# First dense product in Strassen's block form as a stage of its own; queries next; second dense product last

## The chip, the cores and the metric

The kernel runs on one core of a Trainium2 chip. The metric is the device time of one execution in microseconds (us), lower is better. The engines are named as in the profile: PE (TensorE, matmuls), DVE (VectorE), ACT (ScalarE), POOL (GpSimd) and SP (the queue that issues the DMAs).

## The reference

Input x has 2048 rows and 640 columns. Two branches are mixed row by row with a gate; everything is float32.

```python
g = sigmoid((x * gate_w).sum(-1, keepdims=True))
# branch a: 32 heads of 20
q, k, v = split(x @ wqkv)
pq, pk = per_head(q, w_phi), per_head(k, w_phi)
phi_q = concat(softmax(pq), softmax(-pq))        # the same for phi_k
kv, z = phi_k^T v, phi_k summed over the rows
a = (phi_q kv / (phi_q z + 1e-6)) @ wo
# branch b
b = silu(x @ w1) @ w2                            # 640 -> 1728 -> 640
out = g * a + (1 - g) * b
```

`x @ w1` is the first dense product, the one with `w2` the second.

## The kernel before

Everything is held transposed: a tile has 128 features (partitions) by 512 rows of x, and the 640 columns of x are 5 chunks of 128. A float32 operand is split into a high part (`split`: a cast on ACT) and a low part (a subtraction on DVE or POOL), and each product is made in three passes (`PASSES`): high x high, high x low, low x high. `w1` has 13 full tiles of 128 features and 64 columns left over, which are stacked as high and low parts and need two passes.

The order of the instructions on PE, DVE, ACT and POOL is written out by hand: inside `inorder(...)` each of these engines keeps the order of the program text. DMAs are issued by SP, in an order that the scheduler chooses.

1. *Keys and values*: 16 tiles of 128 rows. `kv_proj` (L468) projects, `k_spikes`, `k_sums` and `k_split` make the key features, `kv_acc` (L438) and `kv_rest` (L449) sum features times values. Banks `kvp[0]` to `kvp[2]` hold the projection. The weights of the dense products are loaded and split beside it (`load_f`).
2. *Opening of the dense products*: beside tile 15, `h_first` (L531) makes four feature tiles of the first block in `kvp[0]` and `kvp[1]`; then `kv_out` writes the key-value sums out and the gates are made.
3. *Both dense products, block by block*: four blocks of 512 rows. `h_tile` (L515) makes one tile of the first product (15 matmuls) and its SiLU; two tiles later `out_acc` (L697) uses it in five accumulators of the second product. The result times 1-g goes to DRAM (`fb_d`).
4. Beside the last block: query weights (`fused`), tables, and four tiles of queries (12 to 15): `q_proj` (L426), the features `q_feat`, the sums `q_sum` and `q_norm_sum` on DVE, `q_norm` (L790) and `q_mul` (L826) on POOL, small steps in `q_small`.
5. *Steps*: for pairs of query tiles, `t_mm` (L963) transposes, `t_out` (L979) copies to SBUF, `n_mm` (L1031) makes the numerators, `w_mm` (L1069) the product with `wo`, `w_out` adds `fb_d` and stores. `step(u)` interleaves this with the queries of the following tiles. `PB` is the order of the pairs.

## Time and profile before

| | |
|---|---|
| median of 3 runs | 753.37 us (753.12 to 755.64) |
| profiled execution | 753.52 us, span of its trace 751.7 us |
| granted TensorE clock | 1.000 |
| PE busy | 745.9 us, 4187 matmuls |
| DVE, ACT, POOL busy | 345.1, 262.9, 258.8 us |
| moved by DMA | 50.38 MB, mean 67 GB/s |

By stages, from the profile's windows: keys and values to 173.7 us; the opening to 190; the dense products to about 581, the last 51 us of them with queries beside; the steps to the end, 170.7 us. The stages have different limits, so a share of the whole span says little about one of them. The groups of instructions give the mean duration of one instruction, the chain gives the times at which work followed work. A matmul's duration is longer than the distance from it to the next, since matmuls overlap.

### The profile page before, as it was taken

The page shows a single profiled execution, that of the slowest core. Times are in us where ns is not written, and L with a number is a line of the kernel's source. Part 1 is how long each engine was busy: PE and PEld are TensorE (multiplying, and loading weights), DVE is VectorE, ACT ScalarE, POOL GpSimd, SP SyncE. Part 2 cuts the span into 40 slices and gives each one's busy share as a digit, 9 for nine tenths or more (in the row PEclk, how much of TensorE's full clock was granted, in tenths as well). Part 3 has the DMA queues.
Part 4 walks back from the last instruction along what each step waited for, and adds up shares of the span by engine and source line. Part 5 has one row for each costly group of instructions (what it writes and reads, how often), then busy time and mean ns, then how long its engine had stood idle before and what let it go on. Part 6 is the DMA issues. An engine that isn't in the chain of part 4 may idle for free.

```text
span 751.7 us, 10464 instructions
## 1 busy us (share of the span) xinstructions
PE 745.9 (99%) x4187; PEld 649.2 (86%) x4187; DVE 345.1 (46%) x613; ACT 262.9 (35%) x478; POOL 258.8 (34%) x160
## 2 busy tenths in 40 slices
PE   9999999999999999999999999999999999999998
PEld 7888888888888888888888888888897999999997
DVE  5676666676651230112210122123278776776732
ACT  5444433346452311123111221133354434444231
POOL 2488777866200000000000000001057687776540
PEclk9999999999999999999999999999999999999999
DMA  8111111103660130001300025014002233121222
GB/s 258 53 54 53 54 53 54 58 16 102 185 204 14 37 118 1 1 0 53 105 0 1 0 50 142 35 37 139 15 1 97 78 106 101 57 70 44 72 84 79
DMA packets 35500, 50.38 MB, mean 67 GB/s; under 512 B 3545, under 2 KB 23273, under 8 KB 35451
## 3 DMA queue, kind: packets, MB, share of 16 engines
q1 hardware_dynamic: 35162, 49.19, 21.0%
q8 instruction: 33, 0.54, 0.3%
q10 hardware_dynamic: 288, 0.51, 0.3%
q14 instruction: 17, 0.13, 0.1%
HBM read 38.58 MB, written 11.11 MB: 66 GB/s over the span
## 4 chain that ended last, share of the span: by engine, by line
PE 95%; POOL 2%; DVE 1%; ACT 1%; issue 1%; DMA 1%; SPq 0%; POOLq 0%
PE acc L697 25%; PE ph L515 23%; PE kvp L468 16%; PE pa L1069 9%; PE pq L426 8%; PE pn L1031 3%; PE kv L438 3%; PE pT L963 2%; PE kvp L531 2%; PE kvp L327 1%; PE kvq L327 1%; PE pwk L316 1%; PE pwq L236 1%; POOL eq L826 1%; DMA wvr<-wv 1%
## 5 line engine op out<-in xcount | busy, mean ns | idle before, releaser
L122 POOL TENSOR_TENSOR xb<-xrb,xb 128x512 fp32r<-128x512 f32 (+1 forms) x18 | 20.2, 1147 | 322.1 <-ACT xb L120 322.1
L697 PE MATMUL acc<-u,w 128*128 128x512 f32 x480 | 114.2, 391 | 0.2 <-DVE u L122 0.2
L122 DVE TENSOR_TENSOR u<-ph,u 128x512 fp32r<-128x512 f32 x48 | 33.2, 691 | 175.8 <-ACT u L120 175.7
L697 PEld LDWEIGHTS acc<-u,w 128*128 128x128 f32 x480 | 89.6, 188 | 19.1 <-DVE u L122 0.6
L515 PE MATMUL ph<-xf,w 128*128 128x512 f32 x420 | 99.3, 389 | 0.0
L517 ACT ACTIVATE ph<-ph 128x512 f32<-128x512 f32 x48 | 27.9, 582 | 190.8 <-PE ph L515 190.7
L468 PE MATMUL kvp<-wh,xa 128*128 128x500 f32 (+1 forms) x420 | 93.3, 358 | 0.0
L515 PEld LDWEIGHTS ph<-xf,w 128*128 128x128 f32 x420 | 78.8, 188 | 16.3
L468 PEld LDWEIGHTS kvp<-wh,xa 128*128 128x128 f32 x420 | 71.5, 188 | 10.0
L1069 PE MATMUL pa<-oT,wo 128*128 128x256 f32 x600 | 77.8, 283 | 0.0
L1069 PEld LDWEIGHTS pa<-oT,wo 128*128 128x128 f32 x600 | 74.2, 189 | 0.8 <-ACT oT L1040 0.8
L697 PE MATMUL acc<-u,f 128*128 128x512 f32 x300 | 71.8, 390 | 0.0
L515 PE MATMUL ph<-xf,f 128*128 128x512 f32 x300 | 71.3, 389 | 0.0
L515 PEld LDWEIGHTS ph<-xf,f 128*128 128x128 f32 x300 | 56.3, 188 | 11.7
L697 PEld LDWEIGHTS acc<-u,f 128*128 128x128 f32 x300 | 56.2, 188 | 11.6
L790 POOL TENSOR_TENSOR ez<-eq,zbc 128x1280 f32<-128x1280 f32 x16 | 47.1, 2946 | 41.1 <-ACT eq L776 41.1
L122 POOL TENSOR_TENSOR ph<-ek,ph 128x1280 fp32r<-128x1280 f32 x16 | 47.4, 2962 | 28.5 <-ACT ph L120 28.5
L426 PE MATMUL pq<-wq,xb 128*128 128x320 f32 x360 | 55.9, 312 | 0.0
L426 PEld LDWEIGHTS pq<-wq,xb 128*128 128x128 f32 x360 | 52.8, 188 | 2.3 <-issue 1.2
L468 PE MATMUL kvp<-wl,xa 128*128 128x500 f32 (+1 forms) x210 | 47.6, 356 | 0.0
L826 POOL TENSOR_TENSOR eq<-eq,sm 128x1280 f32<-128x1280 f32 x16 | 37.9, 2370 | 23.6 <-DVE sm L820 19.9
L468 PEld LDWEIGHTS kvp<-wl,xa 128*128 128x128 f32 x210 | 36.3, 189 | 5.5
(154 smaller groups left out, 1026.0 us busy)
## 6 DMA issues: line engine op xcount, KB each, us to landing
wr<-w SPq DMA_DIRECT2D x26, 320.0 KB, 3.4
xrf<-xT SPq DMA_DIRECT2D x20, 256.0 KB, 4.0
fb_d<-o SPq DMA_DIRECT2D x20, 256.0 KB, 2.4
y<-fb_d SPq DMA_DIRECT2D x16, 256.0 KB, 3.2
out<-y SPq DMA_DIRECT2D x16, 256.0 KB, 2.4
xra<-xT SPq DMA_DIRECT2D x14, 256.0 KB, 2.7
xrb<-xT SPq DMA_DIRECT2D x12, 256.0 KB, 2.6
wo<-wo SPq DMA_DIRECT2D x5, 320.0 KB, 2.8
```

The source lines that it names most:

```text
L122: eng.tensor_tensor(lo, src, hi.bitcast(F32), op=ALU.subtract)
L327: nc.tensor.matmul(kv_cols(t, lo, hi), x_of(t)[c][:, hx, :], WKV[hw][:, c, lo:hi], start=(opens and hx == 0 and hw == 0), stop=(c == NC - ...
L426: nc.tensor.matmul(dst, xt[c][:, hx, :], w[:, c, hw, lo : lo + n], start=first, stop=(hx == 1 and c == NC - 1))
L438: nc.tensor.matmul(kvt[i // 2][: KF + 1, i % 2], vs[t % VB][:, i, : KF + 1], ph[:, :, ks[i] : ks[i] + P], start=(t == 0 and i % 2 == 0), s ...
L468: nc.tensor.matmul(kv_cols(t, lo, hi), xt[c][:, hx, :], WKV[hw][:, c, lo:hi], start=(n == 0), stop=(n == 3 * NC - 1), skip_group_check=True,)
L515: nc.tensor.matmul(ph, lhs, rhs, start=(n == 0), stop=(n == len(todo) - 1))
L517: nc.scalar.activation(hs, ph, AF.Silu)
L697: nc.tensor.matmul(acc[m], lhs, rhs, start=(f == order[0] and n == 0), stop=(f == order[-1] and n == len(todo) - 1))
L790: nc.gpsimd.tensor_tensor(ez, Q[t]["e"], zbc, op=ALU.mult)
L826: nc.gpsimd.tensor_tensor(groups(q["e"]), groups(q["e"]), spread(q["sm"][:, 2 * H : 4 * H]), op=ALU.mult)
L1031: nc.tensor.matmul(pns[u, gp][jj * HW : (jj + 1) * HW, a, :], KVW[:w, at : at + HW], rhs, start=True, stop=True)
L1069: nc.tensor.matmul(pa[:, a, :], WO[:, c, hw, ds] if c < NG else WOR[:, ds], o[:, ho, c, :] if c < NG else o[:GW, 0, c, :], start=(k == 0), ...
```

## The change

The first product becomes a stage of its own. Feature tiles are taken in six pairs and blocks of rows in two pairs. Four of the five chunks of x form a 2 x 2 block matrix with the pair of blocks, four chunks of w1 with the pair of tiles, and their product is made from seven products of sums and differences (`product`, `operands`) instead of eight; the fifth chunk is added in the ordinary way. `h_pair` makes the seven products in the order 1, 2, 6, 7, 4, 5, 3, with the additions on DVE between them. The sums of weights are made on POOL (`w_sums`), those of x once for each pair of blocks, on DVE and POOL. Tile 12 and the 64 columns left over stay in ordinary form (`h_std`, with "l" and "r"). SiLU tiles are stored to DRAM (`u_d`).

The queries of tiles 8 to 11 come next, with the ordinary tiles of blocks 2 and 3 between them; then the steps, whose result now goes to `fb_d`; and last the second product, which loads and splits the SiLU tiles, multiplies by 1-g and adds `fb_d` (`o_mm`, `o_out`). `PB` starts with pair 4, and w1's odd tiles are rolled by 256 columns in the host's layout. The core of the diff (a line of "..." where lines are left out):

```diff
-PB = (NP - 2, NP - 1, *range(NP - 2))
+PB = (4, 5, 6, 7, 0, 1, 2, 3)
+NQ = NF // 2
...
+    def w_load(n):
+        p = n % NQ
+        e = wslot(f"wr{n}")
+        s = wslot(f"wt{n}")
+        nc.sync.dma_start(e[:, :D], w1[2 * p])
+        nc.sync.dma_start(e[:, D:], w1[2 * p + 1])
+        WR[n] = e, s
+
+    def w_sums(n):
+        e, s = WR[n]
+        a = [e[:, i * 2 * P : (i + 1) * 2 * P] for i in range(2)] + [e[:, 4 * P : D]]
+        b = [e[:, D + i * P : D + j * P] for i, j in ((3, 5), (0, 2), (2, 3))]
+        o = [s[:, i * P : j * P] for i, j in ((0, 2), (2, 4), (4, 6), (6, 8), (8, 9))]
+        for k, x, y, op in (
+            (0, b[0], b[1], ALU.add),
+            (1, o[0], a[0], ALU.subtract),
+            (2, a[0], b[0], ALU.subtract),
+            (3, a[1], o[1], ALU.subtract),
+            (4, a[2], b[2], ALU.subtract),
+        ):
+            nc.gpsimd.tensor_tensor(o[k], x, y, op=op)
+
+    def w_parts(n, k, eng="dve"):
+        e, s = WR[n]
+        t = W.setdefault(n, {})[k] = two(f"ws{n}{k}")
+        if k == "b":
+            split(t[:, 0, : 3 * P], t[:, 1, : 3 * P], e[:, D : D + 3 * P], eng)
+            split(t[:, 0, 3 * P :], t[:, 1, 3 * P :], s[:, : 2 * P], eng)
+        else:
+            parts(t, {"a": e[:, :D], "c": s[:, 2 * P : 6 * P], "d": s[:, 6 * P : 9 * P]}[k], eng)
...
+    def u_out(f, b, src, early=False):
+        o = u_tile(f"u{b}_{f}", early)
+        nc.scalar.activation(o, src, AF.Silu)
+        nc.sync.dma_start(u_d[f, :, b * 512 : (b + 1) * 512], o)
+
+    def r_out(b, src, early=False):
+        o = u_tile(f"u{b}_r", early)[:FR]
+        nc.scalar.copy(o, src[FR:])
+        nc.vector.tensor_tensor(o, src[:FR], o, op=ALU.add)
+        nc.scalar.activation(o, o, AF.Silu)
+        nc.sync.dma_start(u_d[NF, :FR, b * 512 : (b + 1) * 512], o)
...
+    def operands(s):
+        x = XS[s]
+        n1, n2 = x["n"]
+        t = {k: long(x["t"][k]) for k in range(1, 5)}
+        return {
+            1: [("a", 0, n1[0]), ("a", 1, n1[1])],
+            2: [("a", 2, n1[2]), ("a", 3, n1[3]), ("a", 4, n1[4])],
+            3: [("d", 0, n2[2]), ("d", 1, n2[3]), ("d", 2, n2[4])],
+            4: [("b", 0, t[4][0]), ("b", 1, t[4][1]), ("b", 2, n1[4])],
+            5: [("b", 3, t[1][0]), ("b", 4, t[1][1]), ("b", 2, n2[4])],
+            6: [("c", 0, t[2][0]), ("c", 1, t[2][1])],
+            7: [("c", 2, t[3][0]), ("c", 3, t[3][1])],
+        }
+
+    def product(n, k, dst):
+        todo = [(hw, hx, *p) for hw, hx in PASSES for p in operands(n // NQ)[k]]
+        for i, (hw, hx, w, j, x) in enumerate(todo):
+            nc.tensor.matmul(
+                dst, W[n][w][:, hw, j * P : (j + 1) * P], x[:, hx, :], start=(i == 0), stop=(i == len(todo) - 1)
+            )
+
+    def h_pair(n, between, banks=None):
+        s, p = divmod(n, NQ)
+        b0, b1, f0, f1 = 2 * s, 2 * s + 1, 2 * p, 2 * p + 1
+
+        def mm(k):
+            dst = banks.pop(0) if banks else bank(f"p{n}_{k}")
+            product(n, k, dst)
+            return dst
+
+        def add(o, i, j):
+            nc.vector.tensor_tensor(o, i, j, op=ALU.add)
+
+        def after(k):
+            for part in between.get(k, ()):
+                part()
+
+        after(0)
+        p1 = mm(1)
+        q = fu.tile([P, 2, 512], F32, tag="u", name=f"q{n}", bufs=3)
+        nc.scalar.copy(q[:, 0, :], p1)
+        after(1)
+        p2 = mm(2)
+        add(p2, p2, q[:, 0, :])
+        u_out(f0, b0, p2, n == 0)
+        after(2)
+        p6 = mm(6)
+        add(q[:, 1, :], p6, q[:, 0, :])
+        after(6)
+        p7 = mm(7)
+        r = fu.tile([P, 2, 512], F32, tag="u", name=f"r{n}", bufs=3)
+        add(r[:, 0, :], p7, q[:, 1, :])
+        after(7)
+        p4 = mm(4)
+        add(p4, p4, r[:, 0, :])
+        u_out(f1, b0, p4)
+        after(4)
+        p5 = mm(5)
+        add(r[:, 1, :], p5, q[:, 1, :])
+        add(p5, p5, r[:, 0, :])
+        u_out(f1, b1, p5)
+        after(5)
+        p3 = mm(3)
+        add(p3, p3, r[:, 1, :])
+        u_out(f0, b1, p3)
+        after(3)
...
+            h_std("l", kvp[0], n1, range(4), ends=False)
+            h_std("r", kvp[1], n1, range(4), ends=False)
+            for c in (2, 3):
+                n_split(1, c, home[1][:, (c + 2) * 1024 : (c + 3) * 1024].rearrange("p (s d) -> p s d", s=2))
+            h_std("l", kvp[0], n1, (4,), opens=False)
+            u_out(NF - 1, 0, kvp[0], True)
             kv_rest(t - 1, phs[t - 1], True)
             kv_acc(t - 1, phs[t - 1])
             kv_rest_sum(t - 1)
+            less(nc.vector, b11, b12, b11)
+            h_std("r", kvp[1], n1, (4,), opens=False)
             phs[t] = k_split(t, eks[t])
+            r_out(0, kvp[1], True)
+            for c in range(2):
+                cs = slice(c * 512, (c + 1) * 512)
+                less(nc.gpsimd, b12[:, cs], b22[c], b12[:, cs])
+                less(nc.vector, t2[c], b22[c], b11[:, cs])
+            h_std("l", kvp[0], n2, (0, 1, 4, 2, 3))
+            u_out(NF - 1, 1, kvp[0], True)
+            for c in range(2):
+                cs = slice(c * 512, (c + 1) * 512)
+                less(nc.vector, b21[:, cs], b21[:, cs], t2[c])
+            xt_first(1)
+            xt_first(2)
+            h_std("r", kvp[1], n2, range(NC))
+            r_out(1, kvp[1], True)
+            xt_first(3, "pool")
+
+            def key_sums():
+                kv_rest(t, phs[t], True)
+                kv_acc(t, phs[t])
+
+            def gates():
+                kv_out()
+                nc.vector.tensor_scalar_add(g1, g1, 1.0)
+                nc.vector.reciprocal(g, g1)
+                nc.vector.tensor_scalar(g1, g, -1.0, 1.0, op0=ALU.mult, op1=ALU.add)
+                nc.sync.dma_start(kv_d[: KF + 1], kvo[1])
+
+            h_pair(
+                0,
+                {
+                    1: [key_sums],
+                    2: [gates, lambda: xt_first(4)],
+                    6: [lambda: w_load(1), lambda: w_sums(1)],
+                    4: [lambda: w_parts(1, "a"), lambda: w_parts(1, "c")],
+                    5: [lambda: w_parts(1, "b")],
+                    3: [lambda: w_parts(1, "d")],
+                },
+                [kvp[0], kvp[1], kvp[0], kvp[1], kvp[0], kvp[1], kvp[0]],
+            )
...
+    with inorder(PE, DVE, ACT, POOL):
+        for n in range(1, NQ):
+            todo = plan(n)
+            if n == 1:
+                todo[0] += [x_open]
+                todo[3] += [gates_out]
+            if n in (1, 3):
+                i = n // 2
+                todo[0] += [do(t_loads, i)]
+                todo[5] += [do(n_parts, 0, i), do(n_parts, 0, 2 + i), do(t_sums, i)]
+            if n in (2, 4):
+                i = n // 2 - 1
+                todo[1] += [do(t_parts, i, 1, 2)]
+                todo[5] += [do(t_parts, i, 3, 4)]
             if n == 5:
-                WQ = big("wq", 1)
-                zbc = wslot("zbc")
-                nc.sync.dma_start(zbc, kv_d[KF].partition_broadcast(P))
-            if 5 <= n < 5 + GR:
-                gi = n - 5
-                rq = raw(f"wTq{gi}")
-                load_fused(gi, rq[:, :D])
-                for c0, c1 in ((0, 4), (4, NC)):
-                    fused(kvb["bd"], WQ[:, :, 0, :], WQ[:, :, 1, :], gi, rq, bank(f"pwq{gi}_{c0}"), c0, c1)
-            if n == 8:
-                WO = load_wo()
-            if n == 9:
-                KVW = wslot("kvw")
-                make_kvw()
-            if n == 8:
-                xb_load(0)
-                xb_split(0)
-                xb_load(1)
-                xb_split(1)
-                xb_load(2)
-            if 10 <= n < NF:
-                t = 2 * NP - 4 + n - 10
-                q_tile(t)
-                if n < NF - 1:
-                    q_rest(t)
-
-        def acc_mm(m):
-            for f in order[-3:]:
-                out_acc(order, f, us[f], acc, m)
-
-        def acc_out(m):
-            o = fp.tile([P, 512], F32, tag="o", name=f"o{b}_{m}", bufs=2)
-            nc.vector.tensor_tensor(o, acc[m], G1, op=ALU.mult)
-            nc.sync.dma_start(fb_d[m, :, b * 512 : (b + 1) * 512], o)
-
-        if b < NB - 1:
-            for m in range(NC):
-                acc_mm(m)
-                acc_out(m)
-
+                todo[0] += [do(x_raw, 2, 4), do(x_raw, 3, 4), do(x_raw, 3, 2), do(x_raw, 3, 3)]
+                todo[2] += [do(n_parts, 0, 4), do(n_parts, 1, 4)]
+            h_pair(n, todo)
...
+        q_open(8, q_proj(8))
+        q_feat(8)
+        pf = bank("pf2")
+        h_std("l", pf, n1, range(NC))
+        u_out(NF - 1, 2, pf)
+        q_norm(8)
+        q_open(9, q_proj(9))
+        q_sum(8)
+        q_feat(9)
+        pf = bank("pr2")
+        h_std("r", pf, n1, range(NC))
+        more(8)
+        r_out(2, pf)
+        q_norm(9)
+        q_open(10, q_proj(10))
+        q_sum(9)
+        q_feat(10)
+        pf = bank("pf3")
+        h_std("l", pf, n2, range(NC))
+        u_out(NF - 1, 3, pf)
+        more(9)
+        q_norm(10)
+        pf = bank("pr3")
+        h_std("r", pf, n2, range(NC))
+        q_sum(10)
+        q_open(11, q_proj(11))
+        r_out(3, pf)
+        q_feat(11)
         for i in range(4):
             t_mm(0, i, bank)
             t_out(0, i)
+        more(10)
+        q_norm(11)
+        q_sum(11)
...
         on(0, q_mm)
         n_out(0, range(3))
         stack(WOR, wor[:GW, :D], raw("wor_h").bitcast(F32R)[:GW, :D], 2)
-        for p in range(5, 7):
+        for p in (1, 2):
             x_ahead(p)
-        x_next(2)
         on(0, q_logits)
+        more(11)
         on(0, q_norm, q_sum)
         for u in range(1, NP - 1):
             step(u)
         last_steps(NP - 2)
-    closed("psb", "tb", "rawp", "fu", "fq")
+    closed("psb", "tb")
...
+    def o_out(b, m, acc):
+        o = ob.tile([P, 512], F32, tag="o", name=f"o{b}_{m}", bufs=4)
+        nc.vector.tensor_tensor(o, acc[m], G1[b], op=ALU.mult)
+        (nc.gpsimd if b < NB - 1 else nc.vector).tensor_tensor(o, o, ys[b, m], op=ALU.add)
+        nc.sync.dma_start(out[m * P : (m + 1) * P, b * 512 : (b + 1) * 512], o)
+
+    with inorder(PE, DVE, ACT, POOL):
+        k = 0
+        for b in range(NB):
+            o_block(b)
+            acc = [ps.tile([P, 512], F32, tag="acc", name=f"acc{b}_{m}", bufs=8) for m in range(NC)]
+            tail = OF[-3:] if b == NB - 1 else OF[-1:]
+            for f in OF:
+                if b == 0 and f < NF - NC:
+                    o_w(f + NC)
+                o_u_parts(k + 4)
+                if b == 0 and 1 <= f <= NF - NC:
+                    o_w_parts(f + NC - 1)
+                if f not in tail:
+                    for m in range(NC):
+                        o_mm(b, f, m, acc)
+                o_u(k + 5)
+                k += 1
+            for m in range(NC):
+                for f in tail:
+                    o_mm(b, f, m, acc)
+                o_out(b, m, acc)
```

565 lines of the change are left out of this document (304 added, 261 removed).

## The prediction

> **What bounds the kernel now.** I read the page first: its engine shares, its row of tenths, its chain. Then the waits of TensorE, the groups by line, and the chain and the timelines of two stretches.
>
> ```profile
> span 751.7 us, 10464 instructions
> ...
> PE 745.9 (99%) x4187; PEld 649.2 (86%) x4187; DVE 345.1 (46%) x613; ACT 262.9 (35%) x478; POOL 258.8 (34%) x160
> ...
> DVE  5676666676651230112210122123278776776732
> ...
> PEclk9999999999999999999999999999999999999999
> ...
> PE 95%; POOL 2%; DVE 1%; ACT 1%; issue 1%; DMA 1%; SPq 0%; POOLq 0%
> ...
> L515 PE MATMUL ph<-xf,w 128*128 128x512 f32 x420 | 99.3, 389 | 0.0
> ```
>
> ```profile
> PE kvp L327 <- ACT wh L120: 0.8, 2, 0.4
> PE pT L963 <- POOL eq L826: 0.6, 1, 0.6
> ```
>
> ```profile
> 203.62 3.40 PE ph L515 x15
> 207.02 3.40 PE acc L697 x15
> ...
> 611.40 4.40 PE pq L426 x30
> ```
>
> The page, the waits of TensorE (us in total, times, longest) and the chain (start, us). TensorE is never without work for long, its two waits in mid-kernel are 0.8 and 0.6 us in all, and the chain is TensorE's for 95% of the span. So whatever the change takes off TensorE is gained, and whatever idle time it makes there is lost, with no slack between. DVE is light only in the middle (the dense products) and at 5 to 8 tenths at both ends. The price of a matmul must not be taken from the groups: 389 ns is the time from its start to its end, and matmuls overlap. The chain has the pitch: 15 of 512 columns in 3.40 us, 0.227 us each, in both dense products alike; 30 of a query projection in 4.40 us.
>
> **What is removed from TensorE.** Before, a pair of feature tiles and two blocks of 512 rows took 4 x 15 = 60 matmuls in the first product. The block form has seven products of 2+3+3+3+3+2+2 = 18 tile products, three passes each: 54. There are 6 pairs of tiles and 2 pairs of blocks: 12 x 6 = 72 matmuls less, 72 x 0.227 = **-16.3 us**. The odd feature tile and the 64 columns left over keep their 4 x 25 matmuls, the second product its 820. By the 389 ns of the groups it would look like -28.
>
> **What the pairs add beside the matmuls.** A pair now lasts 54 x 0.227 = 12.2 us on TensorE. Beside it stand:
>
> ```profile
> L122 DVE TENSOR_TENSOR u<-ph,u 128x512 fp32r<-128x512 f32 x48 | 33.2, 691 | 175.8 <-ACT u L120 175.7
> L122 DVE TENSOR_TENSOR f<-wr,f 128x640 fp32r<-128x640 f32 x10 | 7.9, 822 | 5.4 <-ACT f L120 5.4
> L517 ACT ACTIVATE ph<-ph 128x512 f32<-128x512 f32 x48 | 27.9, 582 | 190.8 <-PE ph L515 190.7
> L120 ACT CAST f<-wr 128x640 fp32r<-128x640 f32 x10 | 7.0, 729 | 7.6 <-DMA wr<-w 7.3
> L122 POOL TENSOR_TENSOR xa<-xra,xa 128x512 fp32r<-128x512 f32 (+1 forms) x26 | 26.6, 1046 | 17.4 <-ACT xa L120 17.4
> ```
>
> ```profile
> fb_d<-o SPq DMA_DIRECT2D x20, 256.0 KB, 2.4
> ```
>
> DVE: seven additions, 7 x 0.69 = 4.8 us, and the low halves of 2176 weight columns, 3.4 x 0.82 = 2.8; 7.6 in all, 9 where rows of x are split too. ACT: one copy and four SiLU, 5 x 0.58, and 2176 columns, 3.4 x 0.73: 5.4, at most 8. POOL: 1152 columns of weight sums, about 2.4, and in four pairs another 4.4. Everything is under 12.2, and eight banks for seven products give each 8/7 x 12.2 = 14 us to be read, so from the second pair on I cost these at **0**; if that cover failed, each us by which a chain overran would come 11 times. The new traffic (the activated tiles out to DRAM and back) goes through the SP queue behind the weight loads; a store holds one of two buffers for 0.58 + 2.4 us, and products end 2.0 us apart, so two are enough. The tiles were split into high and low halves before as well, that work only moves to the last stage, 0.58 + 0.69 beside 3.40 us of matmuls: 0.
>
> **The opening: tile 15 to the end of the first pair.** Here only two banks, kvp[0] and kvp[1], serve the seven products, and the sums of x are made just before.
>
> ```profile
> 173.66 6.14 PE kvp L531 x27
> 179.91 1.17 PE kv L438 x10
> 182.34 2.95 POOL L122 TENSOR_TENSOR ph<-ek,ph 128x1280 fp32r<-128x1280 f32 x1 [2.39 <-ACT ph L120]
> 187.34 1.67 DVE L566 TENSOR_TENSOR kvm<-kv,kvl 121x240 f32<-121x240 f32 x5 [1.50 <-POOL w L660]
> 189.34 0.60 DVE L569 TENSOR_TENSOR kvm<-kra 121x80 f32<-121x80 f32 x1
> 189.87 1.19 DVE L549 TENSOR_TENSOR u<-ur,u 128x512 fp32r<-128x512 f32 x1
> 190.99 0.67 DVE L674 TENSOR_SCALAR g<-g 128x16 f32<-128x16 f32 x1
> ```
>
> TensorE comes to this point at 173.7 us and has 50 matmuls of the odd tiles (11.3), two rounds of key sums (1.3 each) and product 1 (1.4) ahead of product 2: it is there at 188.9. Product 2 goes into kvp[1], which r_out(1) must have read. Before r_out on DVE stand the sums, and t2 overwrites the rows that POOL's subtraction into b12 reads, so it waits for POOL. POOL begins that after tile 15's key split, which ended at 185.3 before and about 184.2 now (ACT has no SiLU ahead of its cast). Then two subtractions to 186.4; on DVE the second t2 to 187.1, b21 to 188.5, low halves of 1024 and 2 x 512 columns to 191.2, r_out to 191.9: product 2 waits **3.0**. Product 6 waits for ACT's copy of product 1 (which stands behind the cast of t3): 0.1, product 7 for t3 on POOL: 0.4. Product 4 goes into kvp[0], to be read by the addition of product 6, and that stands on DVE behind the key-value output, the gates and t4: from 195.6, 1.67 + 0.4 + 0.60 + 1.1 + 1.3 to 2.4 + 0.69, to about 202, while product 7 ends at 197.3: **4.6**. Sum **8.1 us**. Bounds: 0, if DVE and POOL run a few us ahead of this, as they do before (none of TensorE's waits above stands at these lines); 12, if the second pair's first product falls on kvp[0], whose last content is read 3.7 us after product 3 ends.
>
> **The query stage.** Before, four tiles of queries were done between matmuls of the last block; now only the odd tiles of two blocks (3.40, 2.27, 3.40, 2.27) lie between them.
>
> ```profile
> L793 DVE TENSOR_REDUCE sm<-ez 128x64 f32<-128x1280 f32 x16 | 23.7, 1479 | 9.5 <-POOL ez L790 9.5
> L790 POOL TENSOR_TENSOR ez<-eq,zbc 128x1280 f32<-128x1280 f32 x16 | 47.1, 2946 | 41.1 <-ACT eq L776 41.1
> 571.79 1.75 PE pT L963 x16
> ...
> 577.66 0.66 PE pT L963 x6
> 578.32 2.74 PE pn L1031 x24
> 561.42 1.28 ACT L776 ACT_TABLE_LOAD   x1
> 562.72 1.27 ACT L776 ACTIVATE eq<-eq 128x1280 f32<-128x1280 f32 x1
> 573.87 2.03 ACT L979 COPY fT<-pT 120x512 f32<-120x512 f32 x4
> 578.31 1.48 DVE L793 TENSOR_REDUCE sm<-ez 128x64 f32<-128x1280 f32 x1
> 580.61 0.22 DVE L810 TENSOR_REDUCE sm<-sm 128x32 f32<-128x64 f32 x1 [0.83 <-POOL sm L802]
> 580.87 0.35 DVE L811 RECIPROCAL sm<-sm 128x32 f32<-128x32 f32 x1
> 581.75 2.38 POOL L826 TENSOR_TENSOR eq<-eq,sm 128x1280 f32<-128x1280 f32 x1
> 585.69 0.82 DVE L410 TENSOR_REDUCE mmq<-pq 128x32 f32<-128x640 f32 x1 [0.89 <-PE pq L426]
> 587.89 0.81 DVE L417 TENSOR_TENSOR eq<-mmq,pq 128x640 f32<-128x640 f32 x1
> ```
>
> Count from the start of tile 8's projection. TensorE: 4 x 4.40 + 11.3 = 28.9, then 22 transposes (2.4): 31.4. DVE per tile: features 3.0 to 3.2, two sums of 1.48, small steps 0.6; with POOL's 2.95 and 2.37 between the sums it follows one projection behind and ends tile 11's features at 31.6. ACT: exp to 33.0, four copies of transposes to 35.0, the sums' scale (after DVE, 35.8) to 36.4, two copies to 37.3. The numerators (L1031, 2.74 us) need these copies and end at 38.2 instead of 34.1: **4.1**. Bounds 0 and 7 (five splits of wo, 0.82 each on DVE, fall in here too).
>
> [...]
>
> Next TensorE projects tile 12 and then must transpose tile 11, whose last steps, more(11), the change puts on DVE behind tile 12's features. Those can't begin before the projection ends. So TensorE stands for the features (585.69 to 588.70, 3.0) and for the row of steps from sum to product (578.31 to 584.13, 5.8), less two transposes of tile 10: **8.6 us**. Before, that row of steps of tile 15 lay beside the projection. Bounds 7 and 9: it is a chain with one answer. Queued behind it are the sums of tile 12, which have 20 us of matmuls as cover.
>
> **The last stage and the end.** Second product and loads: 0 (above). The last output tile needs a multiplication and an addition on DVE where there was one short addition, and a larger store:
>
> ```profile
> 748.54 0.42 DVE y L1094
> ```
>
> 2 x 0.69 - 0.42 = **+1.0 us**.
>
> **Sum.** -16.3 + 8.1 + 4.1 + 8.6 + 1.0 = +5.5 us. The profiled execution took 753.5 us (span 751.7 and 1.8 around it), 0.15 above the median of the runs; so 758.9, **759 us**. With the unknown costs at their ends: -16.3 + 0 + 0 + 7 + 1.0 = -8, and -16.3 + 12 + 7 + 9 + 1.0 = +13.
>
> **Rivals.**
> *TensorE comes back slow from its idle times.* At the start stands a row in which TensorE had been idle:
>
> ```profile
> 1.05 3.78 PE L296 MATMUL warm<-ones 128*128 128x512 f32 x8 [1.05 <-DVE ones L166]
> ```
>
> These eight took 0.47 us each, against 0.227: half pace for about 4 us, a loss of 2. The four waits of 3.0, 4.6, 4.1 and 8.6 would each cost up to that: +6, **765 us**. Against it: the granted clock is 9 of tenths in every slice, that first one too, so no row shows what a pause does. [...]
>
> *The opening is covered (not slower).* Mechanism: POOL and DVE finish the sums of x before TensorE asks for kvp[1]. For it: before, nothing waited here, and POOL was idle 2.39 us ahead of its split. Against: my row of DVE work is 3 us late at the first bank and 4.6 at the second. It decides where r_out(1) ends before 188.9 and the addition of product 6 before 197.3; the time is 759 - 8 = **751**. If the numerators don't wait either, only more(11) is left: 753.4 - 16.3 + 8.6 + 1.0 = **747**.
>
> *The pairs don't run at TensorE's pace* (the change saves matmuls and not time): a store waiting for its SiLU holds up loads behind it on SP, or DVE waits for ACT for POOL. Of 1 us in each of 11 pairs: +11, **770**. Against: the 4.6 us left on DVE.
>
> **How the numbers follow.** A measurement of this kernel can tell 0.5% (3.8 us) from no change: 749.6 to 757.1 counts as the same. Forecast (754 to 764): 0.42, of it 0.10 within the bound. Slow return: 0.20. Opening covered: 0.18, of it 0.13 within the bound, 0.05 below. Only more(11) or less: 0.13, faster. Pairs held up: 0.07. So faster 0.18, same 0.23, slower 0.59. Range 744 to 771: it leaves out most of the 0.13 below and of the 0.07 above. The cases above the old time have most of the chance; their own range is 754 to 771.
>
> **What would show it.** TensorE 72 matmuls fewer, and 15 in 3.40 us still; pairs 12.2 us apart; waits of TensorE for DVE (or ACT) at products 2 and 4 of the first pair; a wait of L1031 for ACT's copies; one wait of 8 to 9 us of a transpose for POOL's product of tile 11. I am wrong if the transpose waits under 5 us, if the first pair ends before 203 us, or if pairs are over 13 us apart.

## The result, and the profile after

The changed kernel takes 785.87 us (median of 4 runs, 784.65 to 786.72) against 753.25 us for the kernel before (752.94 to 755.64): 1.0425 times, 95% interval 1.0399 to 1.0451. The forecast was 759 us, with 744 to 771 as its range: the sign was right, the size was not. The profiled execution took 786.72 us, its span 784.9 us.

From the page of the changed kernel: span, busy times, the rows of tenths of TensorE and of its clock, and the chain's shares.

```profile
span 784.9 us, 10979 instructions
...
PE 746.2 (95%) x4115; PEld 645.1 (82%) x4115; DVE 448.2 (57%) x760; ACT 299.6 (38%) x549; POOL 323.4 (41%) x231
...
PE   9999999997699979999975999999999999999997
...
PEclk9999999998899989999987999999999999999999
...
PE 48%; DVE 4%; DMA 3%; POOL 1%; ACT 1%; issue 1%; SPq 1%; DVEq 0%; POOLq 0%; ACTq 0%
```

TensorE runs 72 matmuls fewer (4115 against 4187) and is busy for longer, 746.2 us against 745.9. Its idle time, span less busy, went from 5.8 to 38.7 us. The row of tenths shows where: at the opening (slices 10 and 11), at 275 to 295 us and in the query stage (slices 21 and 22). The clock, full in every slice before, is below it at the same places (8 of tenths, and 7 in the query stage). The chain could be followed back only to 320 us here (its shares add up to 59%), so its 48% for TensorE can't be set against the 95% of before.

The waits of TensorE (us in total, times, longest):

```profile
PE pT L1106 <- POOL eq L937: 8.8, 2, 8.6
PE pT L1106 <- ACT fT L1122: 5.3, 1, 5.3
PE kvp L583 <- DVE u_r L554: 4.2, 1, 4.2
PE kvp L583 <- DVE q L597: 3.7, 1, 3.7
PE p L583 <- ACT u L548: 3.4, 2, 3.1
PE p L583 <- ACT ws6a L117: 3.4, 1, 3.4
PE p L583 <- ACT ws5a L117: 1.6, 1, 1.6
PE p L583 <- DVE ws6a L119: 1.3, 1, 1.3
```

In this order: tile 11's product on POOL (8.6); ACT's copies ahead of the numerators (5.3); three waits of the opening, at product 2 of the first pair, at its product 4 and at product 1 of the second pair (4.2, 3.7, 3.1); and three waits for the split weights of pairs 5 and 6 (6.3). Pairs are counted from 0, as in the names: ws5a is of pair 5.

TensorE's timeline at these places (start, us, engine, line, operation, count, and in brackets the idle time before it):

```profile
192.70 4.21 PE L583 MATMUL kvp<-xn,ws0a 128*128 128x512 f32 x9 [4.22 <-DVE u_r L554]
...
215.47 5.30 PE L583 MATMUL p<-xn,ws1a 128*128 128x512 f32 x15 [3.07 <-ACT u L548]
...
241.84 3.56 PE L583 MATMUL p<-xn,ws3a 128*128 128x512 f32 x15
...
254.09 3.56 PE L583 MATMUL p<-xn,ws4a 128*128 128x512 f32 x15
...
410.39 4.56 PE L1187 MATMUL pn<-fT,kvw 120*64 120x256 f32 x24
414.88 4.67 PE L455 MATMUL pq<-wq,xn 128*128 128x320 f32 x30
...
428.37 2.39 PE L1106 MATMUL pT<-ident,eq 128*120 128x128 f32 x10 [8.60 <-POOL eq L937]
430.40 6.47 PE L455 MATMUL pq<-wq,xn 128*128 128x320 f32 x30
436.71 1.25 PE L1106 MATMUL pT<-ident,eq 128*120 128x128 f32 x10
```

The second thing to see is the duration behind each wait. Nine matmuls take 4.21 us after the first wait, 0.47 each. Fifteen take 5.30 behind a wait of 3.07, and 3.56 in pairs 3 and 4, which nothing holds up and which stand 12.25 us apart. The same projection takes 4.67 us before the wait of 8.6 and 6.47 behind it, ten transposes 2.39 against 1.25. So behind these three waits, of 4.22, 3.07 and 8.60 us, the work was slower than the same elsewhere; the nine matmuls took twice the pitch of 0.227 us.

The granted clock says the same. It is below full in six stretches: 191.8 to 198.6 us, 205.5 to 208.9, 215.7 to 219.1, 283.9 to 290.7, 406.9 to 413.6 and 424.0 to 434.1, with a mean of 0.51 to 0.54 in each. The last of them, and the sum of the six (us, then busy time and count of TensorE, its weight loads, DVE, ACT and POOL, the granted clock, DMA):

```profile
424.00:434.10 10.10, 5.74 (x24) 5.74 (x25) 4.64 (x9) 1.76 (x3) 6.10 (x5) 0.51 0.00 0
...
sum 37.20, PE 28.51 PEld 22.28 DVE 15.66 ACT 13.07 POOL 18.65; mean PE 4.75 PEld 3.71 DVE 2.61 ACT 2.18 POOL 3.11
```

TensorE is busy for 28.5 us of them. At half pace half of that is lost, some 14 us: an estimate.

The 33.2 us between the two spans: -16.3 for 72 matmuls by their pitch, +32.9 of idle time, and +16.6 of busy time above what was due, since 745.9 - 16.3 = 729.6 was due and 746.2 is there. Of these 16.6 some 14 are half pace. Another 1.2 is that the 72 matmuls turn out to be worth 15.1 (e7_less72 below). The rest, a little over 1, stays open.

### The profile page after: what moved, and what is told of

Read it like the earlier page. It is cut to its first block, busy times and chain, and to the rows that moved or that the text cites. A ratio compares the mean times of both kernels' runs of the same rounds, so it can differ in the third digit from the quotient of the medians.

```text
span 784.9 us, 10979 instructions
## 1 busy us (share of the span) xinstructions
PE 746.2 (95%) x4115; PEld 645.1 (82%) x4115; DVE 448.2 (57%) x760; ACT 299.6 (38%) x549; POOL 323.4 (41%) x231
## 4 chain that ended last, share of the span: by engine, by line
PE 48%; DVE 4%; DMA 3%; POOL 1%; ACT 1%; issue 1%; SPq 1%; DVEq 0%; POOLq 0%; ACTq 0%
PE acc L1429 21%; PE pa L1220 9%; PE pq L455 7%; PE p L583 5%; PE pn L1187 3%; PE pT L1106 2%; DMA ur<-u_d 2%; DVE eq L446 1%; POOL eq L937 1%; DVE sm L904 1%; DMA w2rr<-w 1%; DMA u_d<-u 1%; DMA wo<-wo 1%; PE pwq L229 0%; DVE sm L891 0%
## 5 line engine op out<-in xcount | busy, mean ns | idle before, releaser
L1429 PE MATMUL acc<-u,w 128*128 128x512 f32 x780 | 178.3, 389 | 0.4 <-DVE u L119 0.2
L1429 PEld LDWEIGHTS acc<-u,w 128*128 128x128 f32 x780 | 146.3, 188 | 31.5 <-ACT u L117 0.6
L119 DVE TENSOR_TENSOR u<-ur,u 128x512 fp32r<-128x512 f32 x52 | 36.2, 702 | 75.0 <-ACT u L117 74.8
L117 ACT CAST u<-ur 128x512 fp32r<-128x512 f32 x52 | 32.2, 623 | 107.2 <-PE acc L1429 69.1
L548 ACT ACTIVATE u<-p 128x512 f32<-128x512 f32 x44 | 26.3, 599 | 73.6 <-issue 43.9
L270 POOL TENSOR_TENSOR wt<-wr 128x256 f32<-128x256 f32 (+1 forms) x36 | 25.4, 705 | 66.2 <-DMA wr<-w 32.6
L525 POOL TENSOR_TENSOR ek<-ek,st 128x1280 f32<-128x1280 f32 x16 | 37.9, 2369 | 6.6 <-ACT v L316 3.6
L455 PE MATMUL pq<-wq,xn 128*128 128x320 f32 x240 | 38.7, 320 | 0.0
L455 PEld LDWEIGHTS pq<-wq,xn 128*128 128x128 f32 x240 | 37.4, 197 | 1.1 <-issue 0.8
L1106 PE MATMUL pT<-ident,eq 128*120 128x128 f32 (+1 forms) x176 | 24.1, 287 | 14.0 <-POOL eq L937 8.8
```

The lines of the kernel that those rows point to most:

```text
L117: nc.scalar.copy(hi, src)
L119: eng.tensor_tensor(lo, src, hi.bitcast(F32), op=ALU.subtract)
L455: nc.tensor.matmul(dst, xt[c][:, hx, :], w[:, c, hw, lo : lo + n], start=first, stop=(hx == 1 and c == NC - 1))
L525: nc.gpsimd.tensor_tensor(groups(e), groups(e), spread(st[:, 1, :]), op=ALU.mult)
L548: nc.scalar.activation(o, src, AF.Silu)
L1106: nc.tensor.transpose(pT[:w, jj * 256 + k * P : jj * 256 + (k + 1) * P], es[2 * PB[u] + k][:, j * GW : j * GW + w], ident)
```

## The experiments

Each was run beside the kernel before, which took 753.3 to 753.6 us in every group.

### Does half pace come from having been idle?

*One wait alone, in the kernel before (e8_late15)*: tile 15's last steps are put behind the next tile's features, as the change does with tile 11.

```diff
-        q_norm_sum(t)
-        q_small(t)
-        q_mul(t)
 ...
         on(0, q_logits)
+        q_norm_sum(t)
+        q_small(t)
+        q_mul(t)
         on(0, q_norm, q_sum)
```

> The kernel before, with the one move that the change made at this place: the last steps of the last early tile (15) stand behind the features of the next tile. Theory: a wait of 8.6 us at the transposes and 2.6 us of half pace behind it: 753.3 + 11.2 = 764.5. Rival (idle time without slow return): 753.3 + 8.6 = 762. Rival 2 (absorbed, the steps behind have cover): under 757.

*The same with the wait filled (e12_late15_fill)*: 36 matmuls whose result nobody reads are put where TensorE waits.

```diff
+        idle = single("idle")
+        for k in range(36):
+            nc.tensor.matmul(idle..., ones, ones..., start=(k == 0), stop=(k == 35))
```

> The kernel before with tile 15's last steps late (764.3 us in the run without filling) and 36 matmuls of 512 columns, 8.2 us, whose result is not used, in the place of the wait. Theory (half pace comes from having been idle): 764.3 - 2.4 = 762, and the projection behind it takes 4.5 us as elsewhere. Rival: 764 or more, projection as slow as without filling.

Measured: 764.31 us (ratio 1.0142, 1.0120 to 1.0164) and, filled, 761.29 (1.0101, 1.0083 to 1.0118). TensorE's timeline of the first and then of the second:

```profile
594.35 2.39 PE L963 MATMUL pT<-ident,eq 128*120 128x128 f32 x10 [8.54 <-POOL eq L826]
596.39 4.97 PE L426 MATMUL pq<-wq,xb 128*128 128x320 f32 x30
```

```profile
585.04 8.36 PE L1196 MATMUL idle<-ones 128*128 128x512 f32 x36
593.24 0.38 PE L963 MATMUL pT<-ident,eq 128*120 128x128 f32 x2
593.98 1.31 PE L963 MATMUL pT<-ident,eq 128*120 128x128 f32 x10 [0.36 <-POOL eq L826]
595.04 4.65 PE L426 MATMUL pq<-wq,xb 128*128 128x320 f32 x30
```

The transposes wait for the same product in both, until 594. With useless work in the wait they take 1.31 us instead of 2.39, and the time falls by 3.0 us. So at this place the half pace came from TensorE's having been idle. By the medians this one wait cost 3.0 us beyond its length. The price differed from one execution to the next: the four lie 1.6 to 4.6 us above the median of the filled kernel, at mean granted clocks of 0.991 to 0.996 against 1.000, and between the two profiled ones it is 1.7.

The length of the wait alone does not decide in these runs. In e6_all, a run further down, these are the pieces behind a wait of 3.11 us at pair 5 and one of 2.26 in the numerators:

```profile
264.95 3.73 PE L583 MATMUL p<-xn,ws5a 128*128 128x512 f32 x15 [3.11 <-ACT ws5a L117]
...
403.64 1.93 PE L1187 MATMUL pn<-fT,kvw 120*64 120x256 f32 x8 [2.26 <-ACT fT L1123]
```

The first runs near full pace (3.73 us, against 3.56 in a pair that nothing holds up and 3.72 behind the wait of 1.58 us at pair 5 above), the second does not (1.93 us; the same eight take 1.09 in e18_queries). What decides beside the length was not shown.

*The same filling in the changed kernel (e2_fill)*, ahead of the steps:

```diff
         on(0, q_norm, q_sum)
+        idle = single("idle")
+        for k in range(36):
+            nc.tensor.matmul(idle, WQ[:, 0, 0, :P], ..., start=(k == 0), stop=(k == 35))
         for u in range(1, NP - 1):
```

> The changed kernel, which keeps its wait of 8.60 us at tile 11's transposes, with 36 extra matmuls of 512 columns (8.2 us) ahead of them, whose result is not used. They need nothing that is late, so TensorE is busy instead of idle and the order of everything else stays. Theory (TensorE is slowed by having been idle): the projection behind it takes 4.4 us instead of 6.5, transposes 1.3 instead of 2.4, time 785.9 - 2.6 = 783.3. Rival (matmuls are slow there for another reason, such as operands or DMA): 785.9 or more, projection still 6.5 us.

Measured 786.63 us (1.0433, 1.0413 to 1.0453), no gain. Behind the filled wait the projection took 4.65 us instead of 6.47, as expected. From the ten transposes behind the wait to the next ten it is 5.55 us where it was 8.34. But the opening's waits were 1.5 us longer in this kernel, and a new wait of 1.2 us came in the last stage; that the added bank shifts the rotation of banks is a guess at its cause. As a measure of the whole the run is inconclusive.

### The query stage

*Tile 11's last steps early (e1_early11)*: `more(11)` is moved ahead of the output of the numerators.

```diff
         on(0, q_mm)
+        more(11)
         n_out(0, range(3))
 ...
         on(0, q_logits)
-        more(11)
```

> The changed kernel with one move: the last steps of tile 11 (more(11)) stand on DVE and POOL before the numerators' copies and before tile 12's features, as soon as tile 12's projection is issued. Theory (idle time and a slow return from it): the 8.60 us wait of the transpose goes to under 1, and the work behind it, which took 8.3 us for 5.7 us of matmuls at full pace, runs at full pace: 785.9 - 8.3 - 2.6 = 775. Rival (the pace behind a wait has another cause, only the wait counts): 785.9 - 8.3 = 777.6 and the first projection behind it still 6.4 us instead of 4.4. Rival 2 (something else is late at the same place): no gain over 2 us.

*The copies ahead of the numerators (e5_touts)*: `q_feat(11)` stands behind the four transposes and their copies, `q_sum(11)` behind two more transposes.

```diff
-        q_feat(11)
         for i in range(4):
             t_mm(0, i, bank)
             t_out(0, i)
+        q_feat(11)
 ...
-        q_sum(11)
 ...
         t_all(0, range(4, 6))
+        q_sum(11)
```

> The changed kernel with ACT's four copies of transposes put before tile 11's features and exp, and tile 11's first sum moved behind the next two transposes. Theory: the numerators' wait of 5.3 us falls to about 2 and the half pace of numerators and projection behind it (about 2 us by the granted clock) goes: 785.9 - 3 to - 5. Rival (they wait for something else then): within 1.5 us of 785.9.

Measured 776.45 us for the first (1.0302, 1.0287 to 1.0317): 9.4 less, 7.8 of it the wait (8.6 to 0.8); the stretch of half clock behind it is gone too. 781.93 for the second (1.0367, 1.0345 to 1.0389): 3.9 less, the wait ahead of the numerators 2.2 instead of 5.3. So the first wait has the cause that the forecast gave it, and so has most of the second. ACT's timeline in the changed kernel shows what the forecast left out there:

```profile
405.69 1.28 ACT L887 ACT_TABLE_LOAD   x1 [2.87 <-DVE eq L446]
406.99 1.27 ACT L887 ACTIVATE eq<-eq 128x1280 f32<-128x1280 f32 x1
```

From the start of tile 8's projection (372.40) the features end at 32.9 us where 31.6 was forecast, and the table load begins only then. So the exp ends at 35.9 instead of 33.0. The exp begins 1.30 us after its load began.

### The matmuls that were saved

*72 matmuls fewer in the kernel before (e7_less72)*: 24 feature tiles are made of four chunks instead of five.

```diff
-for c in range(NC)]
+for c in range(NC - (4 <= f < 10))]
```

> The kernel before, with 72 matmuls of the first product left out (the fifth chunk of x in 24 of its feature tiles), and no block form: what 72 matmuls are worth by themselves. Theory (distance between matmuls, 0.227 us): 753.3 - 16.3 = 737. Rival (duration, 0.389 us): 725. Rival 2 (other engines take over): over 742.

Measured 738.29 us (0.9798, 0.9783 to 0.9812): 15.1 less, 0.21 us for each matmul against a pitch of 0.227. So 72 matmuls are worth 15.1 of the 16.3 us forecast, and the rival (0.389 us each) falls.

### The opening and the pairs

*Another order of DVE's work in the opening (e4_open)*: `r_out(1)` ahead of b21 and the splits of t1 and t2, the gates behind the first pair.

```diff
-            for c in range(2):
-                cs = slice(c * 512, (c + 1) * 512)
-                less(nc.vector, b21[:, cs], b21[:, cs], t2[c])
-            xt_first(1)
-            xt_first(2)
             h_std("r", kvp[1], n2, range(NC))
             r_out(1, kvp[1], True)
+            xt_first(2)
             xt_first(3, "pool")
+            xt_first(1)
 ...
-                    2: [gates, lambda: xt_first(4)],
+                    2: [b21_sum],
 ...
+                    3: [lambda: w_parts(1, "b"), lambda: w_parts(1, "d"), gates],
```

> The changed kernel with the vector work of the opening put in another order: the odd columns' output r_out(1) before the sums and splits of x, the sum b21 after product 2, the split of t4 after the addition of product 6, weight parts b and d and then the key-value output and the gates after product 3. The same work, nothing left out. Theory: the waits at products 2 and 4 of the first pair and at product 1 of the second (4.2, 3.7, 3.1 us) fall from 11.0 to about 3 and the half pace behind them (2.0, 1.7, 1.9 us) goes with them: 785.9 - 8 - 5.6 = 772 (776 if a wait over 3 us is left). Rival (pace not tied to idle time): 778. Rival 2 (the waits go elsewhere, the DVE work is only moved to pair 1): over 782.

Measured 778.65 us (1.0336, 1.0316 to 1.0356). TensorE's waits in it:

```profile
PE kvp L583 <- ACT q L606: 4.5, 1, 4.5
...
PE p L583 <- DVE kvm L647: 1.8, 1, 1.8
...
PE kvp L583 <- DVE u_r L554: 0.7, 1, 0.7
```

The wait at product 2 fell from 4.2 to 0.7, and one of 4.5 came up at product 6, whose bank ACT's copy of product 1 must have read. DVE's and ACT's timelines show why:

```profile
192.36 2.52 DVE L119 TENSOR_TENSOR xs<-rx,xs 128x1024 fp32r<-128x1024 f32 x1 [1.12 <-ACT xs L117]
...
194.97 0.58 ACT L606 COPY q<-kvp 128x512 f32<-128x512 f32 x1 [2.64 <-DVE xs L119]
```

By the program, the copy goes into the buffer of the rows that the split of t1 reads, and the edit has put that split last. So the repair made this wait itself. The opening's waits come to 8.9 us in all (0.7, 4.5, 1.9, 1.8) instead of 11.0, where about 3 was expected: the forecast of 772 missed. The time is that of the first rival, but its ground (pace not tied to idle time) is not: of the 7.2 us gained most are pace (TensorE busy 740.4 instead of 746.2).

Three runs on pairs 5 and 6: *a third store buffer (e3_bufs3; one tile of x moves to another pool to make room)*, *the stores issued by ACT instead of SP (e9_actq)*, and *no subtractions of x on POOL (e10_nosums; it leaves out sums that the result needs)*.

```diff
-        return fu.tile([P, 512], F32, tag="ur", name=name, bufs=2)
+        return fu.tile([P, 512], F32, tag="ur", name=name, bufs=3)
```

> The changed kernel with three instead of two buffers for the SiLU tiles on their way to DRAM (one tile of x is put into another pool to make room). Theory: with two buffers a SiLU waits for a store that lands 3.2 us after its issue, ACT falls behind, and the weight casts of pairs 5 and 6 come late; with three the 6.3 us of waits for the weights of pairs 5 and 6 go to under 1.5 and so does the half pace in pair 6 (1.9): 785.9 - 5 to - 8, 778 to 781. Rival (ACT is held by POOL's sums of x, whose inputs come late, and not by the stores): waits of pairs 5 and 6 stay, time within 1.5 us of 785.9.

```diff
-        nc.sync.dma_start(u_d[f, :, b * 512 : (b + 1) * 512], o)
+        nc.scalar.dma_start(u_d[f, :, b * 512 : (b + 1) * 512], o)
```

> The changed kernel with the stores of the SiLU tiles issued by ACT right behind each SiLU instead of by SP, where they stand in order with the loads. Theory (SP's order: a store that waits for its SiLU holds the weight loads and x loads of the next pairs, so POOL's sums and ACT's casts come late): the waits of pairs 5 and 6 for weights (1.6 + 3.4 + 1.3 us) go to under 1.5 in all, with the half pace in pair 6 (1.9): 785.9 - 5 to - 7 = 779 to 781. Rival (POOL's x sums make ACT late): waits stay, time within 1.5 us. Rival 2 (issuing costs ACT too much, 52 x 0.35 us): slower than 787.

```diff
-            nc.gpsimd.tensor_tensor(o, x, y, op=ALU.subtract)
```

> The changed kernel without the sums and differences of x for the second pair of blocks (8 POOL subtractions per 2 calls left out, the splits take the plain rows instead, so products 4 to 7 of the second half are of other values). Theory of SP's order: the weights come as late as before, waits of pairs 5 and 6 stay over 4 us, 784 to 786. Rival (ACT waits for these POOL sums, and all casts behind it): the waits fall to under 1.5 us and the time to 778 to 781.

Measured 783.61, 795.08 and 782.20 us (1.0395, 1.0550, 1.0378). The waits of TensorE over 0.3 us between 229 and 310 us (to 320 in the second), one fence for each run:

```profile
PE p L583 <- ACT ws6a L117: 2.2, 1, 2.2
PE p L583 <- DVE ws6a L119: 1.9, 1, 1.9
PE p L583 <- ACT ws5a L117: 1.7, 1, 1.7
```

```profile
PE p L583 <- ACT ws5a L117: 3.1, 1, 3.1
PE p L583 <- ACT ws6a L117: 1.7, 1, 1.7
PE p L583 <- DVE ws6a L119: 1.6, 1, 1.6
```

```profile
PE p L583 <- ACT xn L117: 2.7, 1, 2.7
```

Neither a buffer nor the queue of the stores moves the waits much (6.3 before, 5.8 and 6.4 here), though the third buffer gained 2.3 us; this speaks against the theory that loads stand behind stores on SP. Without POOL's subtractions 3.6 of the 6.3 us go. ACT's timeline, two pieces of the changed kernel and one of e10_nosums:

```profile
266.28 0.62 ACT L117 CAST xt<-xr 128x512 fp32r<-128x512 f32 x1 [1.66 <-POOL xr L1027]
...
267.30 0.71 ACT L117 CAST ws5a<-wr 128x640 fp32r<-128x640 f32 x1
```

```profile
290.17 0.60 ACT L548 ACTIVATE u<-p 128x512 f32<-128x512 f32 x1 [3.99 <-DMA u_d<-u]
```

In the changed kernel ACT waits for POOL ahead of a cast of xt, and its cast of pair 5's weights comes behind that and a SiLU. The last 2.7 us of e10_nosums stand behind another cast of x. By the timeline that cast, at 292.88, is late because two SiLU ahead of it waited 3.99 and 1.14 us for a store; a store took 3.3 us to land in that run (median of 52), where the forecast had 2.4. In the changed kernel a SiLU ahead of pair 6's casts waits 1.95 us for a store (281.68). So by the timelines POOL's sums and the two store buffers both have a part; a run with both repairs was not made. The second run is 9 us slower than the changed kernel: each store that ACT issues takes it 0.33 us, which lie in an idle time of about 0.4 between a SiLU and the cast behind it. That this makes up the 9 us was not tried.

### All repairs together

*All four (e6_all: e1, e3, e4, e5)*, *with the stores on ACT (e11_best: e1, e3, e4, e9)*, *without the copies (e15_open_early11: e1, e3, e4)*.

> All four moves together (tile 11's last steps, three store buffers, the opening's order, the copies): theory 785.9 - 11 - 7 - 13.6 - 4 = 750, which is just below the kernel before (753.3); rival (pace not tied to idle time): 785.9 - 8.3 - 5 - 8 - 3 = 761.

> Tile 11's last steps early, the opening's order, three store buffers and the stores on ACT together; tile 11's copies left where the change had them. Theory: the gains of the single moves add, 785.9 - 9.4 - 7.2 - 7 = 762. Rival (the gains overlap, as in the run of all four): 767 to 772. Either way above 753.

> The kernel after with the opening's order, three store buffers and tile 11's last steps early, without the change of the numerators' copies. Theory (what the parts gave alone adds up as long as the numerators' wait stays where it is): 785.9 - 7.2 - 2.3 - 9.4 = 767. Rival (no better than all four together, 771.8): 770 to 773.

Measured 771.79 (1.0243), 777.60 (1.0326) and 768.26 us (1.0200, 1.0184 to 1.0216). By what the single runs gained or lost 763, 776 and 767 were due, so in the last two the parts add up to within 1.5 us. With the copies early as well (the first) it is slower than the last by 3.5: the numerators wait 2.3 us instead of 5.0, and the wait at tile 11 is back at 5.7 us, now behind DVE's sum, which waits 5.84 us for POOL's product. Here a wait taken out of a chain of two engines shows the other engine's.

### The block form against the new order

The opening and the pairs had no repair that took their waits away. So *ordinary products in the new order (e13_plain)*: four products of 15 matmuls for each pair, no sums; and *the same with tile 11's last steps early (e14_plain_early11)*.

```diff
-        p1 = mm(1)
...
-        add(p3, p3, r[:, 1, :])
-        u_out(f0, b1, p3)
+        u_out(f0, b0, mm(1, "a", 0), n == 0)
+        u_out(f1, b0, mm(2, "b", 0))
+        u_out(f1, b1, mm(3, "b", 1))
+        u_out(f0, b1, mm(4, "a", 1))
```

> The new order of stages with the first dense product in ordinary form: four products of 15 matmuls for each pair of tiles and blocks instead of seven of 6 to 9, no sums of x and none of weights; everything else as in the kernel after. Theory (the block form brings the waits of the opening, 11.0 us, and of pairs 5 and 6, 6.3, with the half pace behind them, about 10, and saves 16.3): 785.9 + 16.3 - 27 = 775, so 772 to 778, and what is left against the kernel before (about 21) is the query stage with its 5.3 + 8.6 and its half pace. Rival (the waits belong to the order of stages, since splitting, loading and storing are the same in both forms): the 72 matmuls come back and the waits stay, 801 to 803.

> The same ordinary first product, and tile 11's last steps moved ahead of the output of the numerators, as in the early11 run. Theory: less by the 9.4 us of that run, 763 to 768. Rival (nothing else waits in this stage order, so all of the query stage's loss goes): within 3 us of the kernel before, 751 to 757.

Measured 771.57 us (1.0241, 1.0223 to 1.0259) and 761.70 (1.0114, 1.0096 to 1.0132). Page and waits of the first:

```profile
span 770.2 us, 10786 instructions
...
PE 750.0 (97%) x4187; PEld 652.8 (85%) x4187; DVE 370.3 (48%) x639; ACT 276.0 (36%) x493; POOL 247.2 (32%) x149
```

```profile
PE pT L1053 <- POOL eq L881: 8.6, 1, 8.6
PE pT L1053 <- ACT fT L1069: 5.0, 1, 5.0
```

Nothing waits in the opening or the pairs now, and the query stage's two waits are still there. This splits the 33.2 us between the spans. The new order costs 18.5: idle time from 5.8 to 20.2, and 4.1 of half pace (TensorE busy 750.0 us against 745.9 for the same 4187 matmuls). The block form costs 14.7: idle time from 20.2 to 38.7, and TensorE busy 3.8 less where 16.3 less was due, 12.5 too much. Some 10 of these are half pace (the 14 above less the 4.1), 1.2 the smaller worth of the matmuls. The rival (the waits of the opening and the pairs belong to the order) falls.

### Block form where its sums have cover

*Block form for the second pair of blocks alone (e16_second_half)*, with e1's edit: pairs 0 to 5 in ordinary form, and the sums of x and weights for pairs 6 to 11 made beside them. *A third store buffer there (e17_second_half_bufs3).*

> The run with ordinary products and tile 11's last steps early, but with the six pairs of the second pair of blocks in block form, whose sums of x and of weights can be made while the first six pairs run at 13.6 us each with POOL idle. 36 matmuls less than that run: 36 x 0.227 = 8.2 us. Theory (the block form costs time only where its sums come just before their use): no wait of TensorE between 173 and 370 us, 761.7 - 8.2 = 753.5, so 752 to 755. Rival (pair 6's waits of 3.4 and 1.3 come with the block form itself, since its weights need ACT, DVE and POOL in a row, with the half pace behind them): 758 to 761.

> The same with three buffers for the stores instead of two. Theory (stores don't hold up the pairs once POOL's sums have cover): within 1 us of the run with two. Rival (ACT's SiLU waits for a store buffer in each pair and makes the weights late): 2 us less or more.

Measured 753.71 (1.0002, 0.9993 to 1.0011) and 753.78 us (1.0000, 0.9991 to 1.0009). Windows of the first, the stages of the dense product (us, then busy time and count of TensorE, its weight loads, DVE, ACT and POOL, the granted clock, DMA):

```profile
200.00:282.00 82.00, 82.00 (x364) 67.81 (x363) 20.49 (x31) 31.73 (x58) 28.35 (x26) 1.00 0.54 173
282.00:300.00 18.00, 18.00 (x91) 15.28 (x90) 11.69 (x21) 8.84 (x18) 4.81 (x8) 1.00 0.66 198
300.00:362.00 62.00, 62.00 (x321) 53.13 (x320) 38.40 (x67) 30.16 (x59) 13.00 (x16) 1.00 0.48 150
```

TensorE is never idle between 173 and 362 us, with the same sums, casts and products in the second half. Against e14_plain_early11, which differs by the block form in the second half alone, it is 8.0 us faster, and 36 matmuls by their pitch are 8.2. So there the block form costs nothing: its sums are made beside pairs that need none. In the changed kernel pair 6, one of these six, waits 3.4 and 1.3 us, and there the pairs before it have sums of their own to make. That cover would also carry the first six pairs was not tried. The kernel is level with the one before: 36 matmuls less (-8.2) against 5.3 us of waits and 2.0 of half pace at the numerators (4.82 us for 24 matmuls that take 2.81 later), and the end (1.5).

*A shorter chain for tile 11 (e18_queries)*: the copies early, tile 10's product on DVE, tile 11's small steps on DVE.

```diff
+        q_feat(11)
+        q_norm_sum(10)
+        q_small(10)
         q_norm(11)
         q_sum(11)
+        q_mul(10, nc.vector)
```

> The run with the block form in the second half alone, and in its query stage ACT's copies of the first transposes ahead of tile 11's features, tile 10's product on DVE instead of POOL, and tile 11's small steps on DVE. Theory (what is left there is a chain: tile 11's exp to 386.7 us, POOL's product to 389.6 or 390.3, sums and small steps on DVE to 393.1, POOL's product to 395.5, where the transposes now start at 398.7): 3.2 us less, 753.7 - 3.2 = 750.5, so 749.5 to 752, which is below the kernel before by 0.2 to 0.5%. Rival (the wait only moves, as it did when all four changes were made together): 753 to 756.

Measured 753.14 us (0.9994, 0.9985 to 1.0003), not to be told from the kernel before. DVE's and POOL's timelines:

```profile
387.98 3.44 DVE L950 TENSOR_TENSOR eq<-eq,sm 128x1280 f32<-128x1280 f32 x1
```

```profile
387.13 2.95 POOL L914 TENSOR_TENSOR ez<-eq,zbc 128x1280 f32<-128x1280 f32 x1
```

The rival came: the wait of 4.0 at the numerators went, and one of 3.9 at tile 11 came. DVE's product took 3.44 us: POOL's ran beside it for 2.10 us, until 390.08, and from there DVE needed 1.34. Whether the two held each other up was not shown: no run here gives DVE's product alone. No version beat the kernel before. The block form within the old order of stages was not tried.

## Why the prediction was wrong

What held. The matmuls: 16.3 by the pitch, 15.1 when they alone were taken away. The wait of tile 11: 8.6 forecast, 8.60 measured, in the changed kernel and again in e8 (8.54) and e13 (8.6). The places of the waits at product 2, product 4 and the numerators, and who ends them. Pairs 2 to 4 at 12.25 to 12.36 us. The sign.

What failed, by size. The spans are 33.2 us apart and the forecast was 5.5, so the miss is 27.7. *Half pace* is the step that failed, with some 14 us (16.6 is the whole busy time above what was due): the sum put what follows a wait at nothing. It was a rival at 0.20, priced at 6 for four waits of up to 2 us each. Its mechanism was right where it was tried alone (e8 against e12); its chance and its price were too low. The runs showed six stretches of half clock, up to some 3 us lost in each by the same estimate, and one wait of 8.5 us alone cost 3.0. "No row shows what a pause does" was no evidence against it: the kernel before had no pause. The row of the clock reads 9 even in the slice in which eight matmuls took 0.47 us each, so it could not speak against it either. One row spoke for it, the row of those eight matmuls.

*The pairs at 0* (6.3 us). The cover was reckoned by sums of busy time: 7.6 us of DVE and 5.4 of ACT in 12.2. The cover failed by order: ACT does its casts in turn, a cast of x waited for POOL, POOL for DVE's split of x, and the weights of the next pair stood behind it. The forecast named this ("DVE waits for ACT for POOL") and gave it 0.07. It happened at pairs 5 and 6, not in every pair: they began 13.97 and 15.92 us after the pair before, which is one of the three signs of being wrong that the prediction named. By the timelines the two store buffers, which the forecast held to be enough, have a part in pair 6 as well.

*The opening* (11.0 us against 8.1). The first wait was 4.2 instead of 3.0, the second 3.7 instead of 4.6, and the third, 3.1, is the bound that had been left out of the sum: the second pair's first product does fall on a bank that is read late. *The numerators* waited 5.3 instead of 4.1, with the table load in front of the exp (1.28 us) left out of the count. *The end* cost 1.5 instead of 1.0: the work on DVE as forecast, and 0.5 more from DVE's end to the end of the span. With the 16.6 these make nearly all of the 27.7: 16.6 + 6.3 + 2.9 + 1.2 + 0.5 = 27.5.

By parts of the change: the forecast had 13.7 for the new order (numerators, tile 11, end) and -8.2 for the block form with its opening. Measured were 18.5 and 14.7. The order was nearly right; the block form was judged by its matmuls. That a wait of 4 to 6 us stays in the query stage in two arrangements (e6, e18) lies with the chain of DVE and POOL for tile 11 by their timelines; an arrangement without it was not found.

## What to carry to other kernels

Where TensorE is busy for 99% of the time, price each wait that a change brings as its length plus the half pace that may follow (here 3.0 us behind a wait of 8.5), and look for a run or a row that shows that price. A row that has no pause in it is no evidence that a pause is free. Cover is not a sum of busy times: follow each engine's order and ask which instruction of the next step stands behind one that waits. Fewer operations on the bounding engine pay where the extra preparation has a stretch of its own, as e16 shows (8.0 us for 36 matmuls).

## What the runs showed of the hardware

A wait of 3.07 us was followed by 15 matmuls in 5.30 us instead of 3.56 (the changed kernel, granted clock 0.54 between 215.7 and 219.1 us), one of 2.26 by eight in 1.93 (e6_all; 1.09 in e18_queries); a wait of 1.58 us was followed by 15 in 3.72 (the changed kernel, granted clock 1.00 between 268.0 and 271.8 us), one of 3.11 by 15 in 3.73 (e6_all). Behind the wait of 8.6 us ten transposes and 30 matmuls took 2.9 us longer than the same elsewhere (2.39 and 6.47 against 1.25 and 4.67), at a granted clock of 0.51 until 434.1 us. The four executions of e8_late15, whose trace has a wait of 8.54 us, took 1.6 to 4.6 us more than the median with the wait filled (e12_late15_fill). Matmuls whose result is thrown away kept the pace up there: 1.31 us for the ten transposes instead of 2.39, 3.0 us gained by the medians. An exp began 1.30 us after its table load of 1.28 began. A store issued by ACT took that engine 0.33 us, in an idle time of about 0.4 (e9_actq). Two elementwise products of 128 x 1280 on DVE and POOL, 2.10 us of them at once, took 3.44 and 2.95 us (e18_queries).
